# The partial sums of an MLP are loaded through GpSimd's DMA queue in place of SyncE's

## The chip, the core and the metric

The kernel runs on one core of a Trainium2 chip. The core has five engines, each with its own instruction stream that it executes strictly in order: TensorE (PE in the profile; its weight loads are PEld), VectorE (DVE), ScalarE (ACT), GpSimd (POOL) and SyncE (SP). DMA transfers are issued by an instruction of one of these streams; an instruction that must wait for a semaphore holds up everything behind it in its stream. The metric is the time of one execution in device microseconds; lower is better.

## The reference

Attention with a learned decay, then two MLPs, all in float32:

```python
scores = q @ k.T / sqrt(D)                    # 4 batches, 8 heads, 576 positions, 64 wide
scores = where(causal, -1e9, scores + minimum(-(cum_i - cum_j), 0))   # cum = cumsum(max(s, 0))
x = softmax(scores) @ v                       # -> 2304 tokens x 512
h = x @ w_in;  x = (h * sigmoid(1.702 * h)) @ w_out           # first MLP, 512 -> 2048 -> 512
h = x @ w_in2; x = (P(h) / (Q(h) + 1e-6)) @ w_out2            # second MLP, rational function
```

## The kernel before

Each float32 operand of a matmul is held as two parts, a rounded `hi` and a remainder `lo`, and each product is made of three matmuls (`hi*hi`, `hi*lo`, `lo*hi`). The weights come from memory as raw 8-byte numbers and are converted on the chip into such pairs. One *unit* `u` holds 128 of the 2048 hidden features of a layer: `half` 0 is its part of `w_in`, `half` 1 its part of `w_out`.

**A conversion** (`convert`, lines 489 to 506) loads 512 KB into a buffer `raw` (4 buffers, SP queue, line 493 or 495), then runs ACT lines 497 and 499, DVE lines 500, 501, 502 and 504, ACT line 505 (the `hi` part) and DVE line 506 (the `lo` part). Line 504 is the last one that reads `raw`, so it frees the buffer for the load four conversions later. Units for which there is no room yet are converted into one of two `park` buffers and stored to DRAM (`park`, line 543, POOL queue, two 256 KB stores for each conversion); later `fetch` (line 547, SP queue) loads them back.

**The first MLP** works on 8 blocks of 288 tokens. Its 16 units don't fit at once, so it is done in three parts: units 0 to 4 during the attention (`mlp1_first`), whose sums go to DRAM as `x2p`; then `mlp1_rest` twice, with units 5 to 11 (the first pass, about 330 to 550 us in the profile) and units 12 to 15 (the second pass, to 660 us). In each pass, for each block and each unit: 12 matmuls `h` (line 563) into a PSUM bank (4 of them), the activation (`act1`: ACT line 574, DVE line 575, ACT line 577 for `gh`, DVE line 580 for `gl`), and two units later 12 matmuls (line 587) into four accumulators `a`, one for each quarter `d` of the output (`flush`).

At the end of a block DVE adds the sum so far, `xp`, to each accumulator (line 647), and POOL stores the result (line 648: `x<-xp`). The sum so far is loaded by `sums` (lines 633 to 638) into the same four buffers `xp`, after the third unit of the block; so a load of the next block must wait until the store of the block before has landed. In the first pass the loads come from `x2p`, in the second from the first pass's result, 32 loads each.

The second MLP (`mlp2`, from 660 us) works on 6 blocks of 384 tokens.

**What sets the order.** From the end of the attention on, no order is written out by hand: a scheduler with its own model of the engines and transfers orders the instructions of every engine, PE included. So an edit on one queue can move instructions on the others too. `tick` (line 528) and `queue` decide only after which unit a conversion becomes available to it.

Of the kernel before, what the change touches and what calls it, by code (L numbers as in the profile page):

```python
# [55 lines left out]
class Fused:  # L56
# [566 lines left out]
    def mlp1_rest(self, pool, fs, src, dst, after_unit, at_block, last):  # L623
        nc = self.nc
        nblk = 2 * NB
        pend = []
        xps = {}

        def area(blk, d):
            return np.s_[d * P : (d + 1) * P, blk * HB : (blk + 1) * HB]  # L630


        def sums(blk):
            xps[blk] = []
            for d in range(KD):
                xp = self.spool.tile([P, HB], F32, name="xp", tag="xp", bufs=KD)
                nc.sync.dma_start(xp, src[area(blk, d)])
                xps[blk].append(xp)

        def flush():  # L640
            blk, j, f, g, accs = pend.pop(0)
            for d in range(KD):
                self.out1(accs[d][:, :HB], self.units[1, f], d, g, j == 0, j == len(fs) - 1)
            if j == len(fs) - 1:
                for d in range(KD):
                    xp = xps[blk][d]
                    nc.vector.tensor_tensor(xp, accs[d][:, :HB], xp, ALU.add)
                    nc.gpsimd.dma_start(dst[area(blk, d)], xp)  # L648
            if blk == nblk - 1:
                after_unit(f)  # L650

        for blk in range(nblk):
            b, hb = divmod(blk, 2)
            X = self.X[b]
            c0 = hb * HB
            accs = None
            if blk in at_block:
                at_block[blk]()
            for j, f in enumerate(fs):
                h = self.bank("h", f"h2_{blk}_{f}")  # L660
                for _ in self.stage1(h[:, :HB], 1, f, lambda l, kk: X[:, l, kk, c0 : c0 + HB]):
                    pass
                g = self.act1(pool, h[:, :HB], HB, G_BUFS)
                if last and blk == nblk - 1 and j == len(fs) - 1:
                    self.pre = self.tc.keep_in_program_order(
                        nc.scalar.preload_act_table_set("natural_log_exp_and_others")
                    )
                if len(pend) == 2:
                    flush()
                if accs is None:  # L670
                    accs = [self.bank("a", f"a2_{blk}_{f}_{d}") for d in range(KD)]
                pend.append((blk, j, f, g, accs))
                if j == 2:
                    sums(blk)
                self.tick()
        while pend:
            flush()
# [245 lines left out]
```

## Time and profile before

| | |
|---|---|
| median of 3 runs | 1057.89 us (1056.5, 1057.89, 1062.92) |
| the profiled execution | 1063.09 us; from the first to the last instruction (span) 1061.3 us |
| busy share | PE 97%, PEld 89%, DVE 76%, ACT 68%, POOL 30% |
| mean granted TensorE clock | 0.99 of full speed |
| data moved | 117.31 MB, 111 GB/s over the span |

The profile is one execution. PE is busy 97% of it, but a busy share is a mean over stages with different limits; what an edit in one stage can bring is read in that stage, from the idle time of PE there and from what ended it. An issue of a DMA on SP's queue is shown as `SPq`; waiting in that queue costs time only if somebody waits for what stands behind it.

### The profile page before, as it was taken

The page shows a single profiled execution, that of the slowest core. Times are in us where ns is not written, and L with a number is a line of the kernel's source. Part 1 is how long each engine was busy: PE and PEld are TensorE (multiplying, and loading weights), DVE is VectorE, ACT ScalarE, POOL GpSimd, SP SyncE. Part 2 cuts the span into 40 slices and gives each one's busy share as a digit, 9 for nine tenths or more (in the row PEclk, how much of TensorE's full clock was granted, in tenths as well). Part 3 has the DMA queues.
Part 4 walks back from the last instruction along what each step waited for, and adds up shares of the span by engine and source line. Part 5 has one row for each costly group of instructions (what it writes and reads, how often), then busy time and mean ns, then how long its engine had stood idle before and what let it go on. Part 6 is the DMA issues. An engine that isn't in the chain of part 4 may idle for free.

```text
span 1061.3 us, 19897 instructions
## 1 busy us (share of the span) xinstructions
PE 1030.1 (97%) x7073; PEld 944.9 (89%) x7073; DVE 804.8 (76%) x1874; ACT 724.1 (68%) x1668; POOL 315.7 (30%) x421
## 2 busy tenths in 40 slices
PE   7998999999999899989999999999999999999997
PEld 4766898898999899889999999998999999999996
DVE  6777867766644999786388444898998988989886
ACT  6788978977855675554265234788787777777765
POOL 4445835543420003231001211222222222222222
PEclk8899999999999999999999999999999999999999
DMA  8446465543215648897136546000010010100000
GB/s 183 117 120 171 122 163 146 144 136 84 50 48 223 204 141 285 273 285 246 46 124 209 196 123 241 31 30 31 1 48 13 17 44 1 33 29 1 31 1 30
DMA packets 79755, 117.31 MB, mean 111 GB/s; under 512 B 25728, under 2 KB 63616, under 8 KB 78060
## 3 DMA queue, kind: packets, MB, share of 16 engines
q1 hardware_dynamic: 73288, 96.55, 31.3%
q0 software_dynamic: 6144, 19.19, 5.0%
q8 instruction: 56, 0.92, 0.4%
q14 instruction: 43, 0.35, 0.1%
q10 hardware_dynamic: 224, 0.30, 0.1%
HBM read 75.08 MB, written 32.05 MB: 101 GB/s over the span
## 4 chain that ended last, share of the span: by engine, by line
PE 80%; DMA 7%; ACT 5%; DVE 4%; issue 3%; POOL 1%; SPq 0%; ACTq 0%; POOLq 0%; DVEq 0%
PE h L563 32%; PE a L739 18%; PE a L587 14%; PE s L251 5%; PE O L370 5%; DMA raw<-in_moe_w_out_dram 4%; PE tp L344 3%; DMA stgA<-in_moe_w_in_dram 1%; PE idle L75 1%; DMA raw<-in_moe_w_in_dram 1%; ACT cvx L499 1%; ACT kh L176 1%; PE tk L218 1%; POOL wd L543 1%; DVE cvx L504 1%
## 5 line engine op out<-in xcount | busy, mean ns | idle before, releaser
L563 PE MATMUL h<-x,u 128*128 128x288 f32 x1536 | 233.0, 298 | 7.6 <-DVE g L575 3.8
L587 PE MATMUL a<-gh,u 128*128 128x288 f32 x1024 | 229.8, 299 | 2.3 <-ACT gh L577 2.3
L563 PEld LDWEIGHTS h<-x,u 128*128 128x128 f32 x1536 | 213.0, 189 | 12.6 <-DVE g L575 4.3
L722 POOL TENSOR_TENSOR gl<-u,gh 128x384 fp32r<-128x384 f32 x96 | 105.5, 1099 | 290.3 <-ACT gh L720 261.1
L587 PEld LDWEIGHTS a<-gh,u 128*128 128x128 f32 x1024 | 172.1, 189 | 6.6 <-ACT gh L577 2.5
L563 PE MATMUL h<-y,u 128*128 128x384 f32 x864 | 165.7, 336 | 0.0
L563 PEld LDWEIGHTS h<-y,u 128*128 128x128 f32 x864 | 152.9, 188 | 6.2
L587 PE MATMUL a<-gl,u 128*128 128x288 f32 x512 | 147.7, 295 | 1.0 <-DVE gl L580 1.0
L739 PE MATMUL a<-u,gh 128*128 128x512 f32 x432 | 114.6, 394 | 0.9 <-ACT gh L720 0.9
L304 POOL TENSOR_SCALAR bt<-bt,sm 128x128 f32<-128x128 f32 (+3 forms) x129 | 72.0, 569 | 112.4 <-DVE sm L301 58.0
L574 ACT ACTIVATE g<-h 128x288 f32<-128x288 f32 x128 | 51.4, 406 | 74.7 <-PE h L563 64.3
L648 POOL DMA_DIRECT2D x<-xp x64 | 35.4, 554 | 224.4 <-DVE g L575 95.6
L587 PEld LDWEIGHTS a<-gl,u 128*128 128x128 f32 x512 | 96.3, 188 | 2.1 <-DVE gl L580 1.6
L292 ACT ACTIVATE bt<-bt,mn 128x128 f32<-128x128 f32 (+3 forms) x129 | 74.8, 580 | 29.2 <-DVE mn L285 27.2
L739 PEld LDWEIGHTS a<-u,gh 128*128 128x128 f32 x432 | 80.0, 188 | 14.9 <-ACT gh L720 1.8
L575 DVE SCALAR_TENSOR_TENSOR g<-g,h 128x288 f32<-128x288 f32 x128 | 57.0, 449 | 45.3 <-ACT g L574 44.9
L285 DVE CUSTOM_DVE_ANT_0 bt<-s,mask 128x128 f32<-128x128 f32 (+3 forms) x129 | 62.3, 483 | 36.8 <-PE s L251 30.9
L720 ACT ACTIVATE gh<-u 128x384 fp32r<-128x384 f32 x96 | 50.6, 527 | 57.7 <-DVE u L718 57.6
L251 PE MATMUL s<-k 68*128 68x256 f32 (+2 forms) x192 | 73.4, 387 | 7.3 <-ACT k L176 4.1
L705 ACT ACTIVATE y<-h,cf 128x384 f32<-128x384 f32 x96 | 55.4, 577 | 33.8 <-PE h L563 33.8
L710 DVE SCALAR_TENSOR_TENSOR y<-s,cf,y 128x384 f32<-128x384 f32 x96 | 59.3, 618 | 20.4 <-ACT s L707 19.1
L577 ACT ACTIVATE gh<-g 128x288 fp32r<-128x288 f32 x128 | 55.5, 440 | 28.3 <-DVE g L575 27.4
(117 smaller groups left out, 2112.2 us busy)
## 6 DMA issues: line engine op xcount, KB each, us to landing
raw<-in_moe_w_in_dram SPq DMA_DIRECT2D x24, 512.0 KB
raw<-in_moe_w_out_dram SPq DMA_DIRECT2D x24, 512.0 KB
x<-xp POOLq DMA_DIRECT2D x64, 144.0 KB, 3.1
wd<-park POOLq DMA_DIRECT2D x36, 256.0 KB, 4.5
u<-wd SPq DMA_DIRECT2D x8, 1024.0 KB
x2p<-st SPq DMA_DIRECT2D x32, 144.0 KB
xp<-x2p SPq DMA_DIRECT2D x32, 144.0 KB
xp<-x SPq DMA_DIRECT2D x32, 144.0 KB
```

The source lines that it names most:

```text
L251: nc.tensor.matmul(sc[: c1 - c0, :w], lhsT=q[:, c0:c1], rhs=k[:, j0 : j0 + w], start=m == 0, stop=m == 1,)
L285: nc.vector.tensor_tensor_reduce(bt[:, j0 : j0 + w], sc[:, :w], mask, 1.0, 3.0e38 if i == 0 else mn[:, 0:1], ALU.add, ALU.min, mn[:, i : i ...
L292: ex = nc.scalar.activation(bt[:, :n], bt[:, :n], AF.Exp, bias=mn[:, i : i + 1], scale=-1.0, accum_out=sm[:, col : col + 1],)
L304: nc.gpsimd.tensor_scalar(bt[:, :n], bt[:, :n], inv[:, i : i + 1], 1.0, ALU.mult, ALU.mult)
L563: nc.tensor.matmul(ps_tile, lhsT=u[:, wl, kk * P : (kk + 1) * P], rhs=x(xl, kk), start=(n == 0), stop=(n == 3 * KD - 1),)
L575: nc.vector.scalar_tensor_tensor(g[:, :w], g[:, :w], 1.0, h, ALU.add, ALU.mult)
L577: nc.scalar.activation(gh[:, :w], g[:, :w], AF.Copy)
L587: nc.tensor.matmul(acc, lhsT=u[:, wl, d * P : (d + 1) * P], rhs=g[gl], start=(first and i == 0), stop=(last and i == 2),)
L705: nc.scalar.activation(y, h, AF.Abs, scale=cf[:, 4:5])
L710: nc.vector.scalar_tensor_tensor(y, s, cf[:, 7:8], y, ALU.mult, ALU.add)
L722: nc.gpsimd.tensor_tensor(gl, p, gh.bitcast(F32), ALU.subtract)
L739: nc.tensor.matmul(accs[m], lhsT=g[gl][:, m * P : (m + 1) * P], rhs=u[:, wl, :], start=(f == 0 and i == 0), stop=(f == NF - 1 and i == 2),)
```

## The change

`sums`, which loads the sums so far for both passes of the first MLP, issues its loads on POOL's DMA queue:

```diff
         def sums(blk):
             xps[blk] = []
             for d in range(KD):
                 xp = self.spool.tile([P, HB], F32, name="xp", tag="xp", bufs=KD)
-                nc.sync.dma_start(xp, src[area(blk, d)])
+                nc.gpsimd.dma_start(xp, src[area(blk, d)])
                 xps[blk].append(xp)
```

All other instructions are the same ones as before; their order differs from the last part of `mlp1_first` on, on every engine.

**SP, at the change from block 1 to block 2 of the first pass.** `raw` are the loads of weights to be converted, `xp` those of the sums. Before:

```order
L495 DMA raw_6669<-in_moe2_w_out_dram 128x1024
L637 DMA xp_6132<-x2p_66 128x288
L493 DMA raw_6755<-in_moe2_w_in_dram 128x4x256
L637 DMA xp_6134<-x2p_66 128x288
L637 DMA xp_6136<-x2p_66 128x288
L495 DMA raw_6832<-in_moe2_w_out_dram 128x1024
L637 DMA xp_6138<-x2p_66 128x288
L493 DMA raw_6914<-in_moe2_w_in_dram 128x4x256
```

What stands there now on POOL, where the other rows are the stores of parked units and, above these rows, the four stores of block 1's `xp`; four issues stand between the first of those stores and the first row here:

```order
L637 DMA xp_6132<-x2p_66 128x288
L543 DMA wd2_8_6249<-park_5461 128x512
L543 DMA wd2_9_6424<-park_5461 128x512
L637 DMA xp_6134<-x2p_66 128x288
L637 DMA xp_6136<-x2p_66 128x288
L637 DMA xp_6138<-x2p_66 128x288
L543 DMA wd2_9_6424<-park_5461 128x512
L543 DMA wd2_10_6579<-park_5461 128x512
```

On SP the four raw loads now follow one another with nothing between them. On POOL, which had only stores, park stores now stand behind loads.

**ACT, at the end of block 3 of the first pass.** `g` is line 574 of the activation of block 3's units 8 to 11, `raw` and `cvx` are conversions. Before:

```order
L497 ACTIVATE raw_7162<-raw_7162 128x512
L505 ACTIVATE park_5461<-cvx_6915 128x512
L499 ACTIVATE cvx_7163<-raw_7162 128x512
L574 ACTIVATE g_6451<-h2_3_8_6438 128x288
L497 ACTIVATE raw_7252<-raw_7252 128x512
L574 ACTIVATE g_6483<-h2_3_9_6470 128x288
L499 ACTIVATE cvx_7253<-raw_7252 128x512
L505 ACTIVATE park_5461<-cvx_7008 128x512
L577 ACTIVATE gh_6454<-g_6451 128x288
L577 ACTIVATE gh_6486<-g_6483 128x288
L497 ACTIVATE raw_7337<-raw_7337 128x512
...
L574 ACTIVATE g_6528<-h2_3_10_6515 128x288
```

Now:

```order
L574 ACTIVATE g_6451<-h2_3_8_6438 128x288
...
L499 ACTIVATE cvx_7008<-raw_7007 128x512
L497 ACTIVATE raw_7162<-raw_7162 128x512
L574 ACTIVATE g_6483<-h2_3_9_6470 128x288
...
L499 ACTIVATE cvx_7086<-raw_7085 128x512
L577 ACTIVATE gh_6454<-g_6451 128x288
L497 ACTIVATE raw_7252<-raw_7252 128x512
L577 ACTIVATE gh_6486<-g_6483 128x288
L574 ACTIVATE g_6528<-h2_3_10_6515 128x288
L499 ACTIVATE cvx_7163<-raw_7162 128x512
...
L497 ACTIVATE raw_7337<-raw_7337 128x512
L574 ACTIVATE g_6560<-h2_3_11_6547 128x288
```

Each `g` stands one raw load earlier than before: `g_6483` was behind `raw_7252` and is now behind `raw_7162`; `g_6528` was behind `raw_7337` and is now ahead of it. At the beginning of the pass the move is the other way: ahead of the copy `st<-a7_3` (line 601), which frees the last PSUM bank of `mlp1_first`, there now stand lines 497 and 499 of `raw_5487` too, which were behind it.

**PE, at block 2's unit 8 of the first pass.** The rows are matmuls `h2` of line 563 and the accumulations of units 7 and 8 (`gh_6116` and `gh_6156`; the rows of the other three quarters and of `gl` are left out). Before:

```order
L563 MATMUL h2_2_11_6263<-x1_79,u1_11_5369 128x288 x12
L587 MATMUL a2_2_5_0_6042<-gh_6116,u1_7_5009 128x288
...
L563 MATMUL h2_3_5_6295<-x1_79,u1_5_5005 128x288 x12
L587 MATMUL a2_2_5_0_6042<-gl_6118,u1_7_5009 128x288
...
L587 MATMUL a2_2_5_0_6042<-gh_6156,u1_8_5051 128x288
```

Now:

```order
L563 MATMUL h2_2_11_6263<-x1_79,u1_11_5369 128x288 x6
L587 MATMUL a2_2_5_0_6042<-gh_6116,u1_7_5009 128x288
...
L563 MATMUL h2_2_11_6263<-x1_79,u1_11_5369 128x288 x6
L563 MATMUL h2_3_5_6295<-x1_79,u1_5_5005 128x288 x8
L587 MATMUL a2_2_5_0_6042<-gl_6118,u1_7_5009 128x288
...
L587 MATMUL a2_2_5_0_6042<-gh_6156,u1_8_5051 128x288
...
L563 MATMUL h2_3_5_6295<-x1_79,u1_5_5005 128x288 x4
```

Four of the twelve matmuls of `h2_3_5` moved behind the first use of `gh_6156`: PE runs a little less far ahead with `h`.

## Rows read from the trace of the kernel before

**Rows 1.** Busy us (instructions): PE, PEld, DVE, ACT, POOL; clock, DMA share, GB/s.

```profile
340.00:480.00 140.00, 130.91 (x962) 129.15 (x961) 123.20 (x271) 89.33 (x184) 29.40 (x52) 0.99 0.76 244
480.00:500.00 20.00, 20.00 (x153) 20.00 (x152) 12.54 (x30) 10.31 (x24) 2.17 (x4) 1.00 0.83 281
...
530.00:660.00 130.00, 130.00 (x973) 130.00 (x971) 77.53 (x178) 53.75 (x116) 22.10 (x40) 1.00 0.52 172
660.00:1061.00 401.00, 395.58 (x1982) 356.98 (x1981) 354.03 (x600) 300.99 (x604) 105.52 (x96) 1.00 0.07 26
```

**Rows 2.** Timeline, PE: start us, us, line, operation, count [idle before, releaser].

```profile
364.69 0.54 PE L563 MATMUL h<-x,u 128*128 128x288 f32 x2 [2.08 <-ACT st L601]
...
429.18 0.80 PE L587 MATMUL a<-gh,u 128*128 128x288 f32 x4 [2.26 <-ACT gh L577]
430.27 0.40 PE L587 MATMUL a<-gl,u 128*128 128x288 f32 x1 [0.30 <-DVE gl L580]
...
452.51 0.40 PE L563 MATMUL h<-x,u 128*128 128x288 f32 x1 [1.42 <-DVE g L575]
...
461.48 2.33 PE L563 MATMUL h<-x,u 128*128 128x288 f32 x12 [2.37 <-DVE g L575]
```

**Rows 3.** Timeline, ACT: conversions that waited, and the activations behind them.

```profile
427.59 0.65 ACT L497 ACTIVATE raw<-raw 128x512 int32<-128x512 uint32 x1 [6.25 <-DMA raw<-in_moe_w_in_dram]
...
428.70 0.43 ACT L577 ACTIVATE gh<-g 128x288 fp32r<-128x288 f32 x1
...
449.73 0.68 ACT L497 ACTIVATE raw<-raw 128x512 int32<-128x512 uint32 x1 [2.14 <-DMA raw<-in_moe_w_in_dram]
450.30 0.39 ACT L574 ACTIVATE g<-h 128x288 f32<-128x288 f32 x1
...
458.79 0.67 ACT L497 ACTIVATE raw<-raw 128x512 int32<-128x512 uint32 x1 [5.15 <-DMA raw<-in_moe_w_out_dram]
```

**Rows 4.** Timeline, SP's queue: start us, duration us of the issue.

```profile
420.83 0.33 SPq L637 DMA_DIRECT2D xp<-x2p  x1
421.32 0.38 SPq L493 DMA_DIRECT2D raw<-in_moe_w_in_dram  x1
...
423.06 0.43 SPq L495 DMA_DIRECT2D raw<-in_moe_w_out_dram  x1
...
451.43 0.33 SPq L637 DMA_DIRECT2D xp<-x2p  x1
452.16 0.33 SPq L495 DMA_DIRECT2D raw<-in_moe_w_out_dram  x1
```

**Rows 5.** Timeline, DVE: line 504, the last reader of a raw buffer.

```profile
418.12 0.68 DVE L504 CUSTOM_DVE_ANT_0 cvx<-raw,cvx 128x1024 uint16<-128x1024 uint16 x1
...
419.46 0.68 DVE L504 CUSTOM_DVE_ANT_0 cvx<-raw,cvx 128x1024 uint16<-128x1024 uint16 x1
...
451.41 0.68 DVE L504 CUSTOM_DVE_ANT_0 cvx<-raw,cvx 128x1024 uint16<-128x1024 uint16 x1
```

**Rows 6.** Waits of SP's queue, whole kernel: us in total, times, longest.

```profile
SPq L637 <- DMA x<-xp: 134.7, 35, 19.0
SPq L493 <- DVE cvx L504: 76.9, 19, 6.6
```

**Rows 7.** Busy time by stretch, columns as in rows 1: the clock after 461 us.

```profile
461.00:467.00 6.00, 5.52 (x30) 5.52 (x31) 6.00 (x14) 4.58 (x10) 2.34 (x4) 0.72 0.86 261
```

**Rows 8.** Timeline, ACT: the conversion right behind the copy of line 601.

```profile
364.54 0.69 ACT L497 ACTIVATE raw<-raw 128x512 int32<-128x512 uint32 x1
365.12 0.67 ACT L499 ACTIVATE cvx<-raw 128x512 f32<-128x512 f32 x1
```

**Rows 9.** Line 648, POOL's stores of xp: us from issue to landing.

```profile
DMA to landing us min/median/max: 2.0/3.1/7.5
```

**Rows 10.** Line 543, park stores on POOL: issue ns, first and last start; waiters.

```profile
L543 POOL DMA_DIRECT2D wd<-park x36: 539/539/796, 406.6 to 479.1; - x36
...
  DVE park L506: 0.9, 1
```

## The prediction

> **What bounds the kernel now.** I read the profile from the outside in. First, the busy time of each engine by stretch [rows 1]: TensorE (PE) has no idle time from 530 us to the end of the first MLP, and 5.4 us of 401 in the second MLP. In the stretch 340 to 480 us, where the first pass over weight tiles 5 to 11 runs and most weights are still being converted, it is busy 130.9 us of 140: 9.1 us idle. The change touches only the first MLP's loads, so a gain must come out of these 9.1 us and what hangs on them.
>
> Second, the timeline of PE, for where those 9 us lie [rows 2]: four waits carry 8.1 us of them. 2.08 us at 362.6 (PE needs the last PSUM bank of the stage before, which ScalarE has still to copy out), 2.26 at 426.9 (`gh`, from ScalarE), 1.42 at 451.1 and 2.37 at 459.1 (both an `h` whose PSUM bank VectorE has not yet read). A fifth cost follows the last: from 461 to 467 the granted clock is 0.72 of full speed, so part of the stretch ran at the lower level of 1.2 GHz right after PE had stood still; 30 matmuls ran in 6.0 us where 153 in 20 us are normal, that is 16 fewer, or 2.1 us [rows 1, 7]. The ceiling of any gain is 9.1 + 2.1 = 11.2 us, 1.05%.
>
> Third, what is late behind each wait: the timeline of ScalarE (ACT) [rows 3]. In front of every `g` or `gh` that PE waited for stands a conversion (line 497) that itself waited for raw weights: 6.25 us until 427.59, 2.14 until 449.73, 5.15 until 458.79. ACT works in order, so a late raw load stops the activations behind it.
>
> Fourth, why the raw loads are late: the timeline of SyncE's queue (SP) beside VectorE (DVE) [rows 4, 5]. A raw load may be issued when DVE's line 504 has read the buffer's last content. Two line-504 instructions end at 418.12 + 0.68 = 418.80 and 419.46 + 0.68 = 420.14, but the two loads go out at 421.32 and 423.06: 2.5 and 2.9 us late, because an `xp` load that waits for a store of the block before stands ahead of them until 420.83. This is the stall that the change aims at. At 452.16 it is different: the line 504 that frees that buffer ends at 451.41 + 0.68 = 452.09, so the load goes out 0.07 us later although an `xp` load had waited just ahead of it. Of SP's 134.7 us of waiting on line 637 [rows 6], most is in the later, idle part of the queue and costs nothing.
>
> **The change part by part.** The 64 loads leave SP and stand on POOL; the scheduler then orders all engines anew from the first pass on.
>
> 1. The stall at 426.9. Both raw loads can go 2.5 us sooner, so ACT's wait ends near 425.1 in place of 427.59 and `gh` comes 2.5 us sooner, against 2.26 + 0.30 us of stall. But PE has four fewer `h` matmuls ahead of this point in the new order (the excerpt of PE), 4 x 20/153 = 0.5 us, and arrives that much sooner. Worth 2.6 - 0.5 = 2.1 us.
>
> 2. The stalls at 451.1 and 459.1 and the slower clock, 1.42 + 2.37 + 2.1 = 5.9 us. SP didn't cause them. What changes is the order on ACT: the `g` that held PE at 451.1 now stands one raw load earlier, and so does the first of the two after 458.79 (the excerpt of ACT). 36 stores at two for each conversion between 406.6 and 479.1 make 4.0 us for a conversion [rows 10], more than either wait. So the most is 5.9, the least 0 (the conversions are as slow as now, and a wait turns up elsewhere, since ACT has as many conversions in all). I take two thirds, 4.0, since both places gain a whole conversion.
>
> 3. The stall at 362.6. In the new order one more conversion stands in front of the copy that PE waits for. The pair of lines 497 and 499 took 365.12 + 0.67 - 364.54 = 1.25 us [rows 8]; its raw load had already landed at 364.54, just when the copy ended. I add 1.2; the bounds are 0 (load and conversion done sooner) and about 4 (a load as late as at 426.9).
>
> 4. POOL. 32 more issues in the first pass at 0.54 us [rows 10] (a load's own issue on POOL is not in the trace; a park store's is the nearest row): 17 us on an engine that is busy 29.4 us of 140 [rows 1], so the issues alone are covered. What isn't free is the wait: `xp` of the next block must wait until a store has landed, 2.0 to 7.5 us after its issue, 3.1 in the middle [rows 9], and now the parked units' stores stand behind it at three block boundaries. About four other issues (2.2 us) stand between store and load, so the usual delay is 3.1 - 2.2 = 0.9 us at each of the three. The two park buffers are nearly tight already: DVE waited once, 0.9 us, for a park store [rows 10]. PE felt (2.26 + 0.30) / 6.25 = 0.41 of ACT's wait at 426.9. So 3 x 0.9 x 0.41 = 1.1 us, bounds 0 and 3 x 7.5 x 0.41 = 9.2 us.
>
> 5. The second pass (530 to 660) has PE full already; there the 134.7 us leave SP without a gain. POOL has nothing else there: with a store every 12.8 us, 3.1 us to land and four issues of 0.54, the loads are in place in time. The second MLP is ordered anew too (two `h` in a row where one and a part stood); PE had next to no wait there before, so I put 0, with 2 us either way.
>
> Sum: -2.1 - 4.0 + 1.2 + 1.1 = -3.8 us. The profiled execution took 1063.1 us (span 1061.3), so it would take 1059.3; the median of the three runs shown is 1057.9, 5 us less than this execution, and the same 3.8 us off it gives **1054.1 us**, 0.4% less.
>
> **The rivals.**
>
> *Nothing reaches PE.* The conversions run at the pace of DVE, ACT and the transfers, and the raw loads freed on SP only wait elsewhere. For it: the load at 452.16 wasn't held by `xp`, DVE is busy 123.2 us of 140 and the DMA engines 0.76 of the time [rows 1]. Against it: 2.5 us of real lateness at 421. Then 2 and 3 don't come either: 1057.9, give or take 2. The Trainium skill, "DMA: Bandwidth & Descriptors", section "Issuing engines are not separate DMA queues", says that starting DMAs from several engines saves only the sequencer's time, since all run on the same 16 DMA engines; by that rule this rival is right, and the wait of an in-order queue at 420.83 is what the rule doesn't count.
>
> *POOL becomes the queue that holds things up (slower).* The `xp` loads' wait for the stores moves to POOL, in front of the park stores; with both park buffers taken, ACT's line 505 and DVE's line 506 wait, and all activations behind them. Price: up to 9.2 us in part 4; with 1.2 from part 3, and without the 4.0 of part 2 (a delayed conversion eats it): -2.1 + 1.2 + 9.2 = +8.3, 1066 us. It decides when a store takes more than about 5 us at each boundary, since three delays of 5 - 2.2 = 2.8 us at 0.41 are 3.4 us, near all that is gained. For it: landings of 7.5 us do occur, under the DMA load of this stretch. Against it: the middle is 3.1.
>
> *All the stalls go.* The ceiling, 11.2 us without part 3's loss: 1047 us. For it: PE, DVE and the DMA engines all have some slack in sum. Against it: DVE would have to be busy 123.2 us of 129, 95%, and the `xp` loads compete for the same DMA engines.
>
> *The descriptor writer starves.* POOL's issues take long while DVE holds something they need. By the rows: 36 park issues in the busiest stretch took 0.539 to 0.796 us [rows 10], so at most 0.26 us each, 32 x 0.26 = 8 us on a mostly idle engine, 1055 us in the end. The Trainium skill, "SBUF — State Buffer", section "SBUF: two separate sides", says that a DMA issued from GpSimd can't have its descriptors written while VectorE runs in a mode that uses two ports, and gives about 3100 ns for one that takes 620 ns alone; by that the 32 loads would cost POOL 79 us more, an estimate from the page's figures, and with 0.41 of it felt by PE the kernel would take some 1090 us. The trace before does not agree: its POOL issues ran beside DVE at 0.8 us at most.
>
> **How the numbers follow.** The forecast (-6 to +0 us) gets 0.45; nothing reaches PE 0.22; POOL holds things up 0.18; all stalls go 0.13; the descriptor writer starves as the page has it 0.02. A measurement of this kernel can tell about 1% from no change, 10.6 us: under 1047.3 or over 1068.5. Only the ceiling case touches the first, with half its chance and some of the forecast's tail, 0.08; the POOL case passes the second in less than half of its cases, with the last rival 0.09. The rest, 0.83, is the same within 1%. The range runs from the ceiling, 1047, to the POOL case, 1066; the likeliest case alone is 1052 to 1058.
>
> **What would show it.** Right: SP's waits on line 637 are gone, and each raw load goes out within 0.2 us of the line 504 that frees its buffer; PE has no wait over 1 us near 427, and fewer near 451 and 459; the granted clock is 1.00 from 460 to 480; the wait in front of the first `h2` matmuls is 3 us or so. POOL shows waits on line 637 with park stores behind them, and DVE's waits for park stores stay under 3 us in sum. Wrong: if ACT's line 505 or DVE's line 506 wait for park stores for more than 5 us in sum, the POOL rival holds; if the raw waits of ACT don't shrink, nothing reached PE; if PE's matmul count in the second MLP falls below some 102 in 20 us, the new order there costs time that I put at nothing.

## The result, and the profile after

The change made the kernel 1.2% slower: 1073.62 us median of 4 runs (1070.7 to 1074.94) against 1060.41 for the kernel before (4 runs), ratio 1.0118, 95% interval [1.009, 1.0146]. The forecast was 1054.1 us with 0.09 for slower by over 1%. The profiled execution took 1074.94 us, its span is 1073.1.

First the busy time by stretch, columns as in [rows 1], which it answers:

```profile
340.00:480.00 140.00, 132.11 (x969) 129.89 (x967) 119.89 (x263) 86.96 (x182) 35.86 (x64) 0.99 0.73 239
480.00:500.00 20.00, 19.42 (x124) 19.21 (x125) 15.30 (x34) 9.58 (x22) 6.70 (x13) 0.83 0.78 261
530.00:660.00 130.00, 130.00 (x971) 130.00 (x971) 77.59 (x178) 54.98 (x119) 40.56 (x74) 1.00 0.52 173
660.00:1061.00 401.00, 392.93 (x1962) 353.33 (x1961) 330.42 (x594) 286.48 (x597) 99.68 (x96) 1.00 0.07 24
340.00:360.00 20.00, 18.02 (x123) 17.58 (x121) 15.18 (x33) 12.65 (x26) 0.00 (x0) 0.91 0.66 208
```

In these two executions pass 1 and pass 2 are a draw: PE is 1.2 us busier up to 480, and pays for it at the end of the pass (480 to 500: 124 matmuls, clock 0.83, where before had 153 at 1.00). The first `h` of the second MLP starts at 652.19 us; before, at 652.31. So in these two traces nothing had been lost by the point up to which the change moved any load; how far one trace can tell that is asked again below. The loss stands behind it, in a stage that has none of these loads: the last matmul ends at 1068.24 instead of 1056.49, and from the first `h` to there the second MLP takes 416.0 us instead of 404.2, **11.9 us** more.

Second, the timeline of PE in the second MLP, the waits in it (idle us and releaser in brackets). Before had one, 0.91 us at 1051.81. After has four pairs of this kind, at 779, 848, 916 and 985, one at each change of block from the second on, and two behind the last `h`:

```profile
847.90 3.39 PE L563 MATMUL h<-y,u 128*128 128x384 f32 x18 [0.66 <-DVE u L714]
852.09 1.64 PE L739 MATMUL a<-u,gh 128*128 128x512 f32 x6 [0.80 <-ACT gh L720]
...
1044.24 4.35 PE L563 MATMUL h<-y,u 128*128 128x384 f32 x24
...
1055.71 2.09 PE L739 MATMUL a<-u,gh 128*128 128x512 f32 x6 [3.00 <-ACT gh L720]
...
1063.87 1.65 PE L739 MATMUL a<-u,gh 128*128 128x512 f32 x6 [2.16 <-ACT gh L720]
...
1067.40 0.84 PE L739 MATMUL a<-u,gl 128*128 128x512 f32 x3
```

The end of the kernel before, the same view: the last `h` ends at 1046.77, one wait, and 36 matmuls behind it.

```profile
1043.64 3.13 PE L563 MATMUL h<-y,u 128*128 128x384 f32 x17
...
1051.81 1.66 PE L739 MATMUL a<-u,gh 128*128 128x512 f32 x6 [0.91 <-ACT gh L720]
...
1055.65 0.84 PE L739 MATMUL a<-u,gl 128*128 128x512 f32 x3
```

The 11.9 us add up from these rows. From the first `h` to the end of the last one after takes 1.9 us longer (396.4 against 394.5): the four pairs of waits are 1.20, 1.46, 1.24 and 1.17, together 5.1 us, less 18 matmuls (4.2 us) that after has put off to the end; 1.0 is not resolved. Behind the last `h` it takes 19.65 us against 9.72: the 18 matmuls put off, 4.2; the waits, 3.00 + 2.16 - 0.91 = 4.25; and a remainder of 1.5, in which slower matmuls lie: behind the wait of 3.00 us part of the stretch runs at 1.2 GHz (granted clock 0.92 from 1040 to 1060, before 1.00; six matmuls in 2.09 us rather than 1.52).

Third, who waits for whom there, from 660 us on. ACT and DVE before:

```profile
ACT gh L720 <- DVE u L718: 57.6, 67, 1.8
ACT y L705 <- PE h L563: 29.7, 24, 1.9
...
DVE y L710 <- ACT s L707: 19.1, 45, 0.7
```

and after (us in total, times, longest):

```profile
ACT gh L720 <- DVE u L718: 116.7, 48, 2.8
...
DVE y L710 <- ACT s L707: 57.7, 74, 1.0
```

Before, ACT waits 24 times for PE's next `h`: it is ahead of PE. After, that row is gone; ACT and DVE wait for each other instead, twice and three times as long. The timeline of DVE shows the form, before:

```profile
811.59 0.62 DVE L710 SCALAR_TENSOR_TENSOR y<-s,cf,y 128x384 f32<-128x384 f32 x1 [0.66 <-ACT s L707]
...
813.16 0.62 DVE L714 SCALAR_TENSOR_TENSOR u<-u,cf,h 128x384 f32<-128x384 f32 x1
813.92 0.62 DVE L710 SCALAR_TENSOR_TENSOR y<-s,cf,y 128x384 f32<-128x384 f32 x1
```

and after:

```profile
803.38 0.71 DVE L710 SCALAR_TENSOR_TENSOR y<-s,cf,y 128x384 f32<-128x384 f32 x1 [0.58 <-ACT s L707]
804.02 0.54 DVE L713 TENSOR_TENSOR u<-u,h 128x384 f32<-128x384 f32 x1
804.59 0.61 DVE L714 SCALAR_TENSOR_TENSOR u<-u,cf,h 128x384 f32<-128x384 f32 x1
805.12 0.55 DVE L713 TENSOR_TENSOR u<-u,h 128x384 f32<-128x384 f32 x1
...
808.23 1.02 DVE L718 SCALAR_TENSOR_TENSOR u<-y,u 128x384 f32<-128x384 f32 x2
810.23 0.68 DVE L710 SCALAR_TENSOR_TENSOR y<-s,cf,y 128x384 f32<-128x384 f32 x1 [0.97 <-ACT s L707]
811.49 0.70 DVE L710 SCALAR_TENSOR_TENSOR y<-s,cf,y 128x384 f32<-128x384 f32 x1 [0.59 <-ACT s L707]
...
819.65 0.71 DVE L710 SCALAR_TENSOR_TENSOR y<-s,cf,y 128x384 f32<-128x384 f32 x1 [0.58 <-ACT s L707]
827.82 0.71 DVE L710 SCALAR_TENSOR_TENSOR y<-s,cf,y 128x384 f32<-128x384 f32 x1 [0.58 <-ACT s L707]
...
836.62 0.61 DVE L710 SCALAR_TENSOR_TENSOR y<-s,cf,y 128x384 f32<-128x384 f32 x1
...
846.12 0.61 DVE L710 SCALAR_TENSOR_TENSOR y<-s,cf,y 128x384 f32<-128x384 f32 x1
```

Before, the second unit of a pair begins (813.92) when the first is past its line 714. The lines of a round are 710, 713, 714, 710, 713, 716, 717, 714, 718, 716, 717, 718: **staggered**. After, they are 710, 710, 713, 714, 713, 714, 716, 717, 716, 717, 718, 718: two units go through each step side by side, so DVE stands still at the end of a pair until ACT has begun the next two, and ACT stands still at the end until DVE has finished both: **lock-step**. The second line 710 of a pair comes at 803.38, 811.49, 819.65, 827.82: 8.15 us a round. PE's own round of two units (24 `h`, 18 `a`) is 8.3 us. So there are 0.15 us to spare in a round. When the input of the next block is scaled as well (lines 689 and 690, between the lines of these rounds), two rounds take 8.80 and 9.50 us, and PE stands still before 847.90 and 852.09.

### The profile page after: what moved, and what is told of

It reads as the page before. It is cut to its first block, busy times and chain, and to the rows that moved or that the text cites. A ratio compares the mean times of both kernels' runs of the same rounds, so it can differ in the third digit from the quotient of the medians.

```text
span 1073.1 us, 20003 instructions
## 1 busy us (share of the span) xinstructions
PE 1034.6 (96%) x7073; PEld 946.5 (88%) x7073; DVE 786.0 (73%) x1874; ACT 711.9 (66%) x1668; POOL 345.4 (32%) x485
## 4 chain that ended last, share of the span: by engine, by line
PE 53%; DVE 22%; ACT 11%; DMA 7%; issue 5%; POOL 2%; SPq 0%; ACTq 0%; POOLq 0%; DVEq 0%
PE h L563 18%; PE a L587 14%; PE a L739 7%; PE s L251 5%; PE O L370 5%; DVE u L714 4%; DVE u L717 4%; DVE y L716 3%; DMA raw<-in_moe_w_in_dram 3%; PE tp L344 3%; DVE u L713 3%; ACT gh L720 3%; ACT y L705 2%; ACT s L707 2%; DVE y L710 2%
## 5 line engine op out<-in xcount | busy, mean ns | idle before, releaser
L587 PE MATMUL a<-gh,u 128*128 128x288 f32 x1024 | 233.3, 301 | 4.8 <-ACT gh L577 4.5
L722 POOL TENSOR_TENSOR gl<-u,gh 128x384 fp32r<-128x384 f32 x96 | 100.6, 1049 | 303.6 <-ACT gh L720 302.5
L563 PE MATMUL h<-y,u 128*128 128x384 f32 x864 | 158.6, 336 | 1.9 <-DVE u L714 1.9
L710 DVE SCALAR_TENSOR_TENSOR y<-s,cf,y 128x384 f32<-128x384 f32 x96 | 65.8, 685 | 59.7 <-ACT s L707 59.7
L497 ACT ACTIVATE raw<-raw 128x512 int32<-128x512 uint32 x48 | 32.8, 684 | 52.4 <-DMA raw<-in_moe_w_out_dram 29.8
```

The lines of the kernel that those rows point to most:

```text
L563: nc.tensor.matmul(ps_tile, lhsT=u[:, wl, kk * P : (kk + 1) * P], rhs=x(xl, kk), start=(n == 0), stop=(n == 3 * KD - 1),)
L587: nc.tensor.matmul(acc, lhsT=u[:, wl, d * P : (d + 1) * P], rhs=g[gl], start=(first and i == 0), stop=(last and i == 2),)
L710: nc.vector.scalar_tensor_tensor(y, s, cf[:, 7:8], y, ALU.mult, ALU.add)
L722: nc.gpsimd.tensor_tensor(gl, p, gh.bitcast(F32), ALU.subtract)
```

## The experiments

Theory A: the loss is the order of the second MLP, a by-product of the scheduling; it has nothing to do with the queue on the chip. Theory B: the queue on the chip costs it (64 more issues and their waits on POOL, loads at other moments). A later splits: A1, PE's order; A2, the lock-step of ACT and DVE. Each kernel ran beside the kernel before. The second-MLP column is from the first `h` to the end of the last matmul, in the one profiled execution.

| kernel | loads on POOL | ACT and DVE, second MLP | ratio to before, 95% interval | first h, us | second MLP, us |
|---|---|---|---|---|---|
| before | 0 | staggered | | 652.3 | 404.2 |
| after | 64 | lock-step | 1.0118 [1.009, 1.0146] | 652.2 | 416.0 |
| e1 | 4 | lock-step | 1.0124 [1.0096, 1.0153] | 648.9 | 416.1 |
| e2 | 60 | staggered | 1.0011 [0.9992, 1.003] | 652.3 | 404.2 |
| e3 | 32 | staggered | 1.0019 [1.0003, 1.0036] | 651.0 | 404.2 |
| e4 | 64 | staggered, PE by hand | 1.0089 [1.0064, 1.0113] | 650.1 | 412.4 |
| e5 | 64 | staggered from block 2, PE by hand | 1.0105 [1.0082, 1.0129] | 652.0 | 412.4 |
| e6 | 0 | staggered, PE by hand | 0.9992 [0.9977, 1.0006] | 648.5 | 404.0 |
| e7 | 0, 32 left out | staggered | 0.9988 [0.9973, 1.0003] | 647.6 | 404.2 |
| e8 | 0 | staggered, PE by hand | 0.9971 [0.9953, 0.9988] | 648.6 | 401.4 |
| e9 | 64 | lock-step, PE by hand | 1.0161 [1.0138, 1.0184] | 652.6 | 418.7 |
| e10 | 64 | staggered | 1.0035 [1.0016, 1.0054] | 652.0 | 405.0 |
| e11 | 0 | staggered | 0.9997 [0.9979, 1.0014] | 652.8 | 405.1 |
| e12 | 0 | as e8 | 0.9969 [0.9955, 0.9983] | 656.5 | 400.5 |
| e13 | 60 | as e8 | 0.9986 [0.9972, 1.0] | 649.2 | 401.8 |

### Four loads moved, four loads kept, pass 1 alone (e1, e2, e3)

e1 is the kernel before with this line:

```diff
-                nc.sync.dma_start(xp, src[area(blk, d)])
+                (nc.gpsimd if last and blk == 7 else nc.sync).dma_start(xp, src[area(blk, d)])
```

e2 is the kernel after with the reverse of it (`nc.sync if last and blk == 7 else nc.gpsimd`), e3 with `nc.sync if last else nc.gpsimd`.

> The kernel before with only the four loads of the last block of pass 2 moved to POOL's queue; the other 60 stay on SP. In the order that results, pass 1, pass 2 and the first nine units of the second MLP have the same rows on PE as the kernel before, and from unit 9 on the second MLP has the rows of the kernel after (two units in lock-step). Theory A (the loss is the order of the second MLP): slower by about 12 us, ratio 1.009 to 1.014, the first h of the second MLP at 652 us as in both, the last matmul of line 739 some 12 us later than before's 1055.4, ACT's gh waiting for DVE some 117 us in sum where before had 57.6. Theory B (the queue on the chip: 64 issues and waits on POOL, and loads at other moments, cost the time): four of 64 loads cost a sixteenth, under 1 us, ratio 1.000 to 1.002.

> The kernel after with only the four loads of the last block of pass 2 back on SP's queue; 60 of 64 stay on POOL. Pass 1 and pass 2 have the rows of the kernel after on PE, the second MLP those of the kernel before. Theory A (order of the second MLP): the whole loss is gone, ratio to before 0.996 to 1.003, PE waits under 5 us from 660 us on as before. Theory B (the queue on the chip): 60 of 64 loads keep 15/16 of the loss, ratio 1.009 to 1.014.

> Loads of pass 1 on POOL, those of pass 2 on SP. Pass 1 has the rows of the kernel after, the second MLP those of before. Theory A: the loss is gone and what is left is the worth of pass 1 alone, 0 by the trace of after (first h of the second MLP at 652.2 against 652.3): ratio 0.997 to 1.002; my prediction's parts 1 to 4 would make it 3.8 us faster, 0.9964. Theory B with pass 1 as the cause: half of the loss or more, ratio 1.006 to 1.012.

Moving 4 loads costs as much as moving 64; moving 60 or 32 costs next to nothing. The second MLP takes 416.1 us in e1 and 404.2 in e2 and e3, to 0.1 us the figures of after and before, and e1's waits there are those of after:

```profile
ACT gh L720 <- DVE u L718: 116.5, 48, 2.6
...
DVE y L710 <- ACT s L707: 57.8, 74, 1.0
```

Theory B as it stands is out: 60 of the loads on POOL don't cost the time. That the last four alone could cost it on the chip is ruled out by e10 below, which has all 64 on POOL. How four loads reach a stage that doesn't use them can be read in the order of DVE where pass 2 ends. Before (line 647 adds the last sums, 710 and 713 are the first activations of the second MLP):

```
L647 TENSOR_TENSOR xp_9046<-a2_7_12_2_8966,xp_9046 128x288
L647 TENSOR_TENSOR xp_9048<-a2_7_12_3_8967,xp_9048 128x288
L710 SCALAR_TENSOR_TENSOR y_9138<-s_9140,cf_73,y_9138 128x384
L713 TENSOR_TENSOR u_9142<-u_9142,h3_0_0_9125 128x384
```

e1:

```
L710 SCALAR_TENSOR_TENSOR y_9138<-s_9140,cf_73,y_9138 128x384
L713 TENSOR_TENSOR u_9142<-u_9142,h3_0_0_9125 128x384
...
L710 SCALAR_TENSOR_TENSOR y_9173<-s_9175,cf_73,y_9173 128x384
L647 TENSOR_TENSOR xp_9046<-a2_7_12_2_8966,xp_9046 128x288
L647 TENSOR_TENSOR xp_9048<-a2_7_12_3_8967,xp_9048 128x288
L713 TENSOR_TENSOR u_9177<-u_9177,h3_0_1_9160 128x384
```

With the last four loads on POOL the scheduler puts the last two sums behind the first activations, as it does in after; in before, e2 and e3 it puts them ahead. That is the first place where the orders of e1 and before part on DVE. Two units later the lock-step is there: in after the third and fourth unit's lines 710 start at 664.95 and 666.21 with nothing between them, in before a line 713 stands between them (665.93, 667.16, 668.28). PE's order is the same in both up to the ninth unit, in pairs; in before the pairs break up at the tenth (PE gets 9 matmuls of `h`, 9 of `a`, 1 of `h`, and so on), in after never. That the scheduler takes the POOL loads to land later in its own model of time is the likely reason; it is argued from the order, not shown.

### PE by hand, one unit at a time (e4, e5)

The kernel after, and

```diff
-                K.mlp2(tp2, lambda i: slots[i] if i < len(slots) else xslot(i), blks)
+                with tc.manual_schedule(engines={mybir.EngineType.PE}):
+                    K.mlp2(tp2, lambda i: slots[i] if i < len(slots) else xslot(i), blks)
```

In e5 the same context is entered only when `i == 1` in `mlp2`, and left behind the last flush.

> The kernel after, all 64 loads on POOL, with PE in the second MLP held to the order in which the code is written (one h of 12 matmuls, then one a of 9, in turn); the first MLP has the same rows as the kernel after, and ACT and DVE of the second MLP are ordered by the scheduler around it, one unit after another. Theory A: no loss, ratio 0.994 to 1.003, with no lock-step of two units and DVE's waits for ACT's line 707 near before's 19 us rather than 58. Theory B: the loss stays, ratio 1.009 to 1.014.

> The kernel after, all 64 loads on POOL, first MLP and first block of the second MLP with the rows of the kernel after; from the second block of the second MLP on, PE is held to the written order (one h of 12 matmuls, one a of 9, in turn). The by-hand kernel e4 had 102 to 103 matmuls in each 20 us from 680 to 1040 us and no wait at a block boundary, but lost its time in the first 20 us (73 matmuls against 105, a wait of 3.9 us for gh and a clock of 0.83), because only three h stand ahead of the first a. Here six do, as in before and after. Theory A (order of the second MLP): the four boundary stalls of 1.1 to 1.5 us, the two waits of 3.0 and 2.2 us behind the last h and the slow clock there go; ratio 0.998 to 1.004 (the change-over from the first block, where three a stand in a row, may cost 1 to 3 us once). Theory B (the queue on the chip): POOL has all 64 loads as in after, the loss stays, 1.009 to 1.014.

Both missed: 1.0089 and 1.0105 lie outside the ranges of theory A and about where theory B put them. But the waits that theory A is about did go: no block change has a wait from 680 us (e4) and 740 us (e5) on, and every 20 us there have 101 to 103 matmuls, up to 1040. The written order itself makes new waits, once each. In e4 the first `a` waits 3.90 us for `gh`, as only three `h` stand ahead of it; in e5 three `a` stand in a row at the change from the scheduler's order to the written one, and PE waits 1.19 and 3.73 us. Behind the waits of 3.90 and 3.73 us part of the stretch runs at the lower level of 1.2 GHz (0.83 and 0.91 of 2.4 GHz in the rows). Busy time of e4 from 660 us, then of e5 from 700:

```profile
660.00:680.00 20.00, 17.72 (x73) 15.15 (x74) 14.04 (x25) 11.94 (x24) 4.66 (x4) 0.83 0.15 63
```

```profile
700.00:720.00 20.00, 18.47 (x88) 15.58 (x86) 18.09 (x32) 14.89 (x32) 4.35 (x4) 1.00 0.14 40
720.00:740.00 20.00, 16.21 (x71) 14.00 (x72) 14.29 (x27) 12.54 (x26) 4.06 (x4) 0.91 0.11 39
```

In e5 that is 15 + 32 matmuls fewer than 103 in 20 us, 9.1 us, more than the whole 8.2 us by which its second MLP is longer than before's. So these two neither confirm nor refute A; they needed a start with six `h` ahead and no change-over.

### PE's order against the order of ACT and DVE (e6, e8, e9)

All three hold PE to pairs of units, as it runs after. In e8 (kernel before) and e9 (kernel after) the edit in `mlp2` is the same:

```diff
+        hand = ExitStack()
         for i, blk in enumerate(blks):
+            if i == 0:
+                hand.enter_context(self.tc.manual_schedule(engines={mybir.EngineType.PE}))
...
-                if len(pend) == 2:
-                    flush()
...
                 pend.append((blk, f, g, accs))
+                if f % 2 and len(pend) == 6:
+                    flush()
+                    flush()
...
+        hand.close()
```

e6 is the kernel before with `i == 1` and `len(pend) == 4`: pairs from the second block on, two units less ahead.

> The kernel before, all 64 loads on SP; from the second block of the second MLP on, PE is held by hand to the order of the kernel after: two h (24 matmuls), then two a (18). ACT and DVE are ordered by the scheduler around it and come out one unit behind the other, not in lock-step. No load moves. Theory A1 (PE's pairs alone cost it): boundary stalls of 1 to 1.5 us each at four or five blocks, ratio 1.005 to 1.01. Theory A2 (it needs ACT and DVE in lock-step, which puts both gh at the end of a pair): no boundary stalls of over 0.5 us, ratio 0.998 to 1.003. Theory B (the queue on the chip): 0.999 to 1.001, as no load moves.

> The kernel before, all 64 loads on SP. PE in the second MLP is held by hand to the order of the kernel after: six h first, then two a, two h, two a in turn, with six units' a (54 matmuls) behind the last h. ACT and DVE are ordered around it by the scheduler and come out one unit behind the other. Theory A1 (PE's order costs it): boundary stalls over 1 us and 5 us of waits behind the last h, ratio 1.008 to 1.013. Theory A2 (ACT and DVE in lock-step cost it): at boundaries under 0.5 us, at most the end is longer by what the 18 further matmuls there have to wait, ratio 0.998 to 1.005. Theory B (the queue on the chip): no load moves, 0.999 to 1.001.

> The kernel after, all 64 loads on POOL, with PE in the second MLP held by hand to the same order as in e8, row for row; here ACT and DVE come out in lock-step of two units as in the kernel after (some ten rows differ from after). Theory A2 (the lock-step of ACT and DVE costs it): as slow as after, ratio 1.009 to 1.014, and against e8, which has the same rows on PE, 6 to 12 us slower. Theory A1 (PE's order): the same as e8, whatever that is. Theory B: 1.009 to 1.014, and e8 at 1.000.

e8 and e9 have the same rows on PE through the whole second MLP. e8 takes 0.9971 of before, e9 1.0161: **20 us apart**, 17.3 of them in the second MLP (401.4 against 418.7). What differs there is the order of ACT and DVE, staggered in e8, in lock-step in e9 (the loads' queue differs as well; e2 and e13, and for the second MLP e10 with all 64 on POOL, show it to be worth next to nothing). So A2 holds and A1 falls: pairs on PE cost nothing (e6, e8) as long as ACT and DVE don't march in pairs. Waits of e8 from 660 us, then of e9:

```profile
ACT gh L720 <- DVE u L718: 38.8, 51, 2.2
ACT y L705 <- PE h L563: 16.9, 16, 1.6
...
DVE y L710 <- ACT s L707: 11.5, 29, 0.4
```

```profile
ACT gh L720 <- DVE u L718: 95.3, 39, 2.7
...
DVE y L710 <- ACT s L707: 57.7, 74, 1.6
```

PE in e9 stands still at all five block changes, 0.58 to 2.30 us at each, and 3.36 us behind the last `h`: 10.6 us of waits in all. At the block changes it waits for the next block's scaled input (lines 689 and 690), where after had waited for lines 714 and 720. Behind the longest waits the granted clock falls to 0.95 (700 to 720 us) and 0.79 (1060 to 1080). How the rest of the 17.3 us is made up is not resolved. e8 has a single wait of 0.81 us at 711, and the 54 matmuls behind its last `h` run without one. I had expected e8 at 0.998 at best; it beats both kernels, what its 2.8 us in the second MLP come from is not shown, and e12, the same kernel in another set of runs on the same chip, repeats it.

### The lock-step undone by a buffer (e10, e11)

e10 is the kernel after, e11 the kernel before, with one more buffer for one tile:

```diff
-        y = new("y", 2)
+        y = new("y", 3)
```

> The kernel after, all 64 loads on POOL, with a third buffer for the tile y of the second MLP and nothing else changed. SP's and POOL's rows are those of after; in the second MLP ACT and DVE come out one unit behind the other, PE in turns of one unit, and three units' a (27 matmuls) are left behind the last h where before has 36 and after 54. Theory A2 (the lock-step of ACT and DVE costs it): loss gone with all loads on POOL, ratio 0.995 to 1.003, no boundary stall over 0.5 us. Theory B (the queue on the chip): 1.009 to 1.014.

> The kernel before, all 64 loads on SP, with the third buffer for y as in e10. The second MLP's order is nearly that of e10 from its second block on. Against e10 it shows what the queue of the loads is worth at the same order of the second MLP: theory A and the trace of after (first h of the second MLP at 652.2 against 652.3) say 0, the two within 0.3% of each other; my prediction's parts 1 to 4 say e10 is 3.8 us faster, 0.36%. Against before: 0.995 to 1.002, as 9 matmuls (2.4 us) fewer stand behind the last h.

With all 64 loads on POOL the second MLP takes 405.0 us and the loss goes from 1.18% to 0.35%; on SP it takes 405.1. A tile that has nothing to do with the loads decides it, as A2 says (on its own e10 doesn't tell A2 from A1, since PE's order changes with it; e8 and e9 do). The ratio of e10 was just outside the 1.003 that I had given. Between the two the order of the second MLP is worth 0.1 us, so the 2.9 us between their medians lie ahead of it or are spread; the next experiment is about that.

### What the loads are worth in the first MLP (e7, e12, e13)

e7 is the kernel before without the 32 loads of pass 1:

```diff
-                nc.sync.dma_start(xp, src[area(blk, d)])
+                if last:
+                    nc.sync.dma_start(xp, src[area(blk, d)])
...
-                    nc.vector.tensor_tensor(xp, accs[d][:, :HB], xp, ALU.add)
+                    if last:
+                        nc.vector.tensor_tensor(xp, accs[d][:, :HB], xp, ALU.add)
+                    else:
+                        nc.vector.tensor_copy(xp, accs[d][:, :HB])
```

e12 is e8 again; e13 is e8 with e2's line for the loads. Their second MLPs have the same rows on PE, ACT and DVE.

> The kernel before without the 32 loads of sums of pass 1 (left out: the sums of the first five weight tiles are not added; VectorE copies the new sums in place of adding). Pass 1 keeps nearly the order of before and the second MLP has exactly before's order. This is the most that any queue for these 32 loads can give in pass 1: SP's waits on them are gone, and their traffic too. If my prediction's parts 1 and 2 were right that the queue's wait is felt by PE: first h of the second MLP at least 2.1 us earlier than 652.3 us, ratio 0.994 to 0.998. If nothing reaches PE (conversions paced by the landing of raw loads and by DVE): first h at 652 give or take 1, ratio 0.999 to 1.001.

> The kernel of e8 again (all 64 loads on SP, PE of the second MLP by hand in pairs), beside e13 on one chip: as e8, 0.9953 to 0.999 of before, if its gain is no accident of one chip; 0.999 to 1.001 if it is.

> The kernel of e8 with 60 of the 64 loads on POOL (the four of the last block of pass 2 stay on SP). The second MLP has the same rows as e12 on PE, ACT and DVE alike, pass 1 those of the kernel after, so the two differ by the queue and by pass 1's order alone. My prediction's parts 1 to 4: 3.8 us faster than e12, ratio to before 0.992 to 0.995. Nothing reaches PE: the two the same within 0.15%. A small loss by the queue (e10 against e11 was 2.9 us): 2 to 4 us slower than e12, about the time of before, first h of the second MLP 2 to 4 us later than e12's.

Even without the loads the kernel gains 0.12%, with an interval that reaches to 0.27% and past zero. Its first `h`, at 647.6, is earlier than the bound that I had set for "felt by PE" (2.1 us before 652.3), but that sign is worth little: as is shown below, the rows of before reach it at 648.5 in another execution. With 60 of them on POOL it takes 1057.34 us against 1056.64 in e12: 0.7 us slower by the medians, 1.8 by the ratios, the intervals overlap. The forecast's 3.8 us faster is refuted; no change and a loss of up to some 3 us are not told apart by this pair.

The four comparisons of loads on POOL with loads on SP at the same or nearly the same order of the second MLP lean one way, though: by the medians e2 is 0.9 us and e3 1.1 us slower than before, e10 2.9 us slower than e11, e13 0.7 us slower than e12. A loss of 1 to 3 us in front of the second MLP is therefore likelier than none; what makes it is open.

The column of the first `h` shows why one trace could not have told it. Six executions have the very same rows on PE and ACT up to there (before, e1, e6, e8, e11, e12; e1 differs by its four loads and two rows of DVE), and their first `h` starts at 652.3, 648.9, 648.5, 648.6, 652.8 and 656.5 us: 8 us of spread, mean 651.3. Eight with the order of after in pass 1 (after, e2, e3, e4, e5, e9, e10, e13) lie between 649.2 and 652.6, mean 651.4. The second MLP repeats to 0.1 us in the order of before (four kernels) and in that of after (two), and to 1.3 us in e8's (three).

## Why the prediction was wrong

**The step that failed** is in part 5: "The second MLP is ordered anew too (two `h` in a row where one and a part stood); PE had next to no wait there before, so I put 0, with 2 us either way." It was 11.9 us. I had seen the new order, and looked only at PE's rows of it. PE in pairs is harmless, as e8 shows. What I did not read is that DVE's and ACT's rows changed as well, from staggered to side by side, and that PE had next to no wait before because ACT was ahead of it (29.7 us of waiting for `h`). That reserve was the thing to price: a pair's round through ACT and DVE against PE's 8.3 us. Of the rivals none had this place, and the range, 1047 to 1066, did not hold the time. The last sentence of the prediction, on a matmul count falling below some 102 in 20 us, named the sign: 840 to 860 has 93 and 980 to 1000 has 93, where before had 101 and 102.

Of the 13.2 us between the medians of the two kernels these 11.9 are the most; the 1.3 left are of the size of the loss in e2, e3 and e13. The forecast lay 19.5 us below the result: 13.2, the gain of 3.8 that didn't come, and 2.5 because the kernel before has a median of 1060.41 with a fourth run, and not 1057.89.

Three readings were off without deciding anything. The 5.4 us of idle PE "in the second MLP" are 0.91 of waiting and 4.5 behind the last matmul (1056.49 to 1061). The 134.7 us are SP's waits in both passes, not in the second alone. And the 2.1 us for the slow clock count again 0.48 us of the wait before (PE is busy 5.52 of the 6 us in [rows 7]).

**Part 1**, the stall at 426.9: right in what it says, as the raw loads now go on time. Line 504 in the trace after, then SP:

```profile
469.50 0.68 DVE L504 CUSTOM_DVE_ANT_0 cvx<-raw,cvx 128x1024 uint16<-128x1024 uint16 x1
```

```profile
470.25 0.33 SPq L495 DMA_DIRECT2D raw<-in_moe_w_out_dram  x1
```

This load goes out 0.07 us after the end of the line 504 ahead of it, and so do all the others from 414 to 475 us (0.05 to 0.07; near the old stall at 424.82 and 426.81), where [rows 4, 5] had 2.5 and 2.9 us. Of the 2.26 us stall 0.29 is left, at 432.5.

**Part 2**, the stalls at 451.1 and 459.1 and the clock: they are gone as well (0.68 us at 458, the clock is 1.00 from 460 to 480), more than the two thirds that I took. But the stalls moved rather than went. PE and ACT after:

```profile
346.68 0.56 PE L587 MATMUL a<-gl,u 128*128 128x288 f32 x1 [1.42 <-DVE gl L580]
...
365.02 7.21 PE L563 MATMUL h<-x,u 128*128 128x288 f32 x53 [2.29 <-ACT st L601]
...
480.58 0.61 PE L587 MATMUL a<-gh,u 128*128 128x288 f32 x1 [2.75 <-ACT gh L577]
```

```profile
477.23 0.66 ACT L497 ACTIVATE raw<-raw 128x512 int32<-128x512 uint32 x1 [3.96 <-DMA raw<-in_moe_w_out_dram]
```

The load issued at 470.25, on time, lands when ACT starts at 477.23, 7.0 us later, and ACT has waited 3.96 for it; PE then waits 2.75, and right behind that wait, with part of the stretch at 1.2 GHz (0.83), it runs 29 matmuls fewer from 480 to 500, 29 x 20/153 = 3.8 us. With the 21 fewer from 340 to 360 (123 against 144, clock 0.91), 2.7 us, that gives back what parts 1 and 2 had gained. That stall belongs to the new order and not to one execution: from 480 to 500 us PE runs 121 to 140 matmuls at a granted clock of 0.83 to 0.91 in the eight executions with the order of after, and 145 to 153 at 1.00 in the six with that of before. ACT's waits for raw weights from 340 to 530, before and then after:

```profile
ACT raw L497 <- DMA raw<-in_moe_w_in_dram: 28.8, 16, 6.2
ACT raw L497 <- DMA raw<-in_moe_w_out_dram: 18.2, 14, 5.2
```

```profile
ACT raw L497 <- DMA raw<-in_moe_w_out_dram: 28.1, 14, 4.0
ACT raw L497 <- DMA raw<-in_moe_w_in_dram: 18.8, 18, 2.1
```

In sum they are 47.0 us before and 46.9 after (43.2 to 47.2 in the six executions, 45.0 to 47.9 in the eight): they "don't shrink", which the prediction gave as the sign that nothing reached PE. For the first MLP that rival was right, or a little too kind, by the small loss above. So was the rule of the Trainium skill, "DMA: Bandwidth & Descriptors", section "Issuing engines are not separate DMA queues", that stood beside it: starting DMAs from several engines saves only the sequencer's time. The trace agrees, with 46.9 against 47.0 us.

**Part 3**, the stall at 362.6: 2.29 us after, 0.2 more and not 1.2 (1.48 to 3.23 in the eight executions, 1.67 to 2.35 in the six).

**Part 4**, POOL: the issues were priced right, the waits came, and no wait of PE for them is seen. Line 637 after:

```profile
L637 POOL DMA_DIRECT2D xp<-x2p x32: 536/541/742, 327.3 to 537.8; - x32
...
  DMA x<-xp: 21.7, 16
```

0.54 us for an issue as forecast, 21.7 us of waiting for stores in 16 places. Park stores stand behind them, but DVE's line 506 waits for one once, 0.9 us, as in [rows 10]. So nothing of the 1.1 us is seen, and the rival of the POOL queue is out as the cause, though the time came out beyond its 1066; at most the small loss above is left for it. The rival of the descriptor writer is out too: the longest issue took 0.74 us, the loads of the first pass landed 5.0 us after their issue (median) and those of the second 2.6, and no line 647 waits for one of them.

**Part 5**, pass 2: right, PE is busy 130.00 of 130 us after as it was before [rows 1].

The sum forecast for the first MLP, -3.8 us, was inside what one execution differs from the next by (8 us at the first `h`), so no single trace could have confirmed it either. I read four stalls of one execution as if they were the kernel's: the stall near 427 is 2.26 us in the trace before and 1.25, 2.14, 1.92, 1.59 and 1.63 in e1, e6, e8, e11 and e12, with the same rows, and a clock under 1.00 between 440 and 480 shows in three of the six (before, e8, e12).

## What to carry to other kernels

Where a scheduler orders the work by a simulated time, an edit of a queue can change the order of a later stage that it doesn't touch: compare the order of every engine there, not of PE alone, and look for units that go side by side where they were staggered. Price a new order by the round of the helping engines against PE's round, and by who waited for whom before; a stage with no wait on PE has a reserve that an order can use up. And a gain of a few us read from the stalls of one execution needs a second execution of the same kernel beside it.

## What the runs showed of the hardware

From 660 to 1061 us DVE is busy 354 us before and 330 after, with 600 and 594 instructions, so the slower kernel has the faster instructions. Lines 718 and 717 differ most, with 96 instructions each in both. Groups by line, before and after (busy us, mean ns):

```profile
L718 DVE SCALAR_TENSOR_TENSOR u<-y,u 128x384 f32<-128x384 f32 x96 | 73.5, 765 | 1.1
L717 DVE SCALAR_TENSOR_TENSOR u<-u,cf,r 128x384 f32<-128x384 f32 x96 | 67.9, 707 | 0.0
```

```profile
L717 DVE SCALAR_TENSOR_TENSOR u<-u,cf,r 128x384 f32<-128x384 f32 x96 | 58.8, 613 | 0.0
...
L718 DVE SCALAR_TENSOR_TENSOR u<-y,u 128x384 f32<-128x384 f32 x96 | 49.1, 553 | 0.0
```

The long ones run beside POOL's `gl`. Before, `gl` runs on POOL at 809.33 for 1.18 us, and the line 718 that starts on DVE at 809.68 takes 1.25 us in place of 0.55. Over the whole second MLP before, the 30 instructions of line 718 that overlap a `gl` take 1.24 us on average and the other 66 take 0.55, and the 48 of line 717 that do take 0.80 against 0.61; lines 713 and 714, whose `h` is in PSUM, show no such difference (0.55 either way; 0.62 and 0.61). In lock-step `gl` falls mostly beside line 710, ahead of which DVE waits for ACT anyway; that line grows from 618 to 687 ns. The Trainium skill, "SBUF — State Buffer", section "SBUF: two separate sides", says that an operation of GpSimd that reads SBUF and one of VectorE with two inputs in SBUF take a shared port pair one after the other, each for its whole length. The trace agrees for these two lines, with the 1.24 against 0.55 us and the 0.80 against 0.61. So a busy share is a poor measure here: 24 us less of it went with 12 us more of time.
